# Attention slots of a three-part kernel: the product with v after both passes over the scores

## The chip, the cores and the metric

The kernel runs on one core of one Trainium2 chip. The metric is the time of one execution in device microseconds (us). Five engines work in it: TensorE (PE in the rows, PEld for its weight loads), VectorE (DVE), ScalarE (ACT), GpSimd (POOL) and SyncE (SP), which issues the DMAs.

## What is computed

The reference runs three layers one after the other on 2 batches of 768 tokens. The first is attention over 8 heads of 64 columns, in which a query sees only the keys of its own cluster; the other two are expert layers on the 1536 x 512 result.

```python
def _attn_ref(q, k, v, centroids):
    q_assign = np.argmax(np.einsum('bhsd,hcd->bhsc', q_n, c_n), axis=-1)   # 16 clusters
    k_assign = np.argmax(np.einsum('bhsd,hcd->bhsc', k_n, c_n), axis=-1)
    mask = q_assign[:, :, :, None] == k_assign[:, :, None, :]
    scores = np.where(mask, scale * np.matmul(q, k.transpose(0, 1, 3, 2)), -1000000000.0)
    attn = np.exp(scores - np.max(scores, axis=-1, keepdims=True))
    attn = attn / (np.sum(attn, axis=-1, keepdims=True) + 1e-09)
    return np.matmul(attn, v)

def reference(**kwargs):
    x = attention output, laid out as (B * S, H * D)
    x = _moe_ref(x, w_in, w_out, a, b)        # x @ w_in, a rational function, @ w_out
    return _moe2_ref(x, phi, w1, w2)          # soft mixture of 8 experts
```

Only the attention stage is touched by the change.

## The kernel before

**Pairs and slots.** Two heads make a pair; there are 8 pairs, and each pair takes 12 slots, so the stage has 96 slots, numbered n = 0 to 95 (slot n belongs to pair n // 12, k = n % 12). The loop runs from n = -10 to 96. A pair goes through two passes over its scores. The first pass finds each row's maximum and sum: `a1_mm` (L380 and L381, four matmuls into a two-bank PSUM tile named s1), `a1_neg` (L390 on VectorE: negate, reduce, write to SBUF) and `a1_exp` (L398 on ScalarE: exponential with its row sum). The second pass computes the scores again, transposed and with maximum and sum folded into the operands: `a2_mm` (L455 and L456, four matmuls into a tile s2), `a2_exp` (L460 on ScalarE, which writes e), and then `a2_av` (L469), the product of v and e. The first pass runs LEAD = 10 slots ahead. So a slot n does the second pass of slot n, the first pass of slot n + 10, and the product with v of slot n - 1. Slots 86 to 96 have no first pass left.

**What the two passes share.** The tiles s1 and s2 come in turn from one pool of two buffers (psS): a first pass waits until L390 has read the first pass before it, and a second pass until L460 has read the second pass before it. e and the negated scores have two buffers each, the accumulator of the product with v (psA) one.

**The small work.** Around these, a table of steps by slot (`plan`) prepares the pair three ahead and decodes the 64-bit weights of the next layer. Its steps on TensorE are called small work here: L248 (scores against the centroids), L263 (transposes of them), L290, L306 and L319 (cluster matrices), L434 (statistics of the first pass turned into rows), L601, L610 and L622 (weights of w_out turned and multiplied by phi). Each writes a tile of a pool of three PSUM buffers (psM), which ScalarE or VectorE reads afterwards. L601, L622 and L263 are transposes that fill 128 rows and 128 columns of the array; the others use fewer rows or columns. The step L253 (`scaled`) on ScalarE reads what L248 wrote and stands one slot later in the table.

**The order.** TensorE, ScalarE, VectorE and GpSimd run in the order in which the code emits, and each does its queue in turn; the loop below sets it. The order of SyncE's DMAs is made by the scheduler. Steps of ScalarE, VectorE and GpSimd of a slot are emitted ahead of its second pass by `run`, those of TensorE (the small work) by `run(n, "P")` at the slot's end. At the end of a half pair (n a multiple of 6) ScalarE also copies the product out of psA (`copy`, L480), and GpSimd splits that copy one or two slots later (L489, L490).

Of the kernel before, what the change touches and what calls it, by code (L numbers as in the profile page):

```python
# [59 lines left out]
def tile_kernel(ctx, tc, qT, kT, v, cenT, cenP, consts, constsb, ab, w_in, w_out, phi, w1, w2, out, dbg=None):  # L60
# [85 lines left out]
    def load(p, names="kq"):  # L146
        b, hp = divmod(p, H // 2)
        r = raws.setdefault(p, {})
        for h in range(2):
            for n in names:  # L150
                if (p, n) == (1, "k"):

                    r[n, h] = dec_p.tile([128, 512, 2], I32, tag="raw64", name="rawk1", bufs=2) \
                        .rearrange("p n t -> p (n t)").bitcast(F32)[:, 0:S]
                else:
                    r[n, h] = raw_p.tile([128, S], F32, tag="raw" + n, name=f"raw{n}{h}", bufs=4 if n == "q" else 2)
                SP.dma_start(r[n, h], (kT if n == "k" else qT)[b, 2 * hp + h])

    def load_v(p):
        b, hp = divmod(p, H // 2)  # L160
        vs[p] = v_p.tile([128, 2, 6, D], F32, tag="v", name="vt")
        SP.dma_start(vs[p], v[b, 2 * hp:2 * hp + 2].rearrange("h (j p) d -> p h j d", p=128))
# [299 lines left out]
    def a2_av(p, k):  # L462
        half, j = divmod(k, 6)
        if j == 0:
            av[p, half] = psA.tile([128, 512], F32, tag="av", name="av")
        a = av[p, half]
        e = es.pop((p, k))
        for h in range(2):
            PE.matmul(a[64 * h:64 * h + 64, 0:HS], vs[p][:, h, j, :], e[:, h, :],  # L469
                      start=(j == 0), stop=(j == 5))  # L470

    def a2_x(p, half):

        b, c = divmod(p, H // 2)
        t0 = b * S + half * HS
        hold = {}

        def copy():
            hold["x"] = s2_p.tile([128, HS], F32, tag="x", name="x", bufs=1)
            ACT.copy(hold["x"], av.pop((p, half))[:, 0:HS])  # L480

        def split():
            done = 0
            while done < HS:
                t, off = divmod(t0 + done, TB)
                n = min(HS - done, TB - off)
                src = hold["x"][:, done:done + n]
                dh, dl = xh[t][:, c, off:off + n], xl[t][:, c, off:off + n]
                POOL.tensor_scalar(dh, src, 1.0, 1.0, ALU.mult, ALU.mult)  # L489
                POOL.tensor_tensor(dl, src, dh.bitcast(F32), ALU.subtract)  # L490
                done += n

        return copy, split
# [150 lines left out]
    def open_w():  # L644
        pctx.close()
        keep = ctx.enter_context(tc.tile_pool(name="keep", bufs=1, reuse_waits="tile"))
        return keep, bctx.enter_context(tc.tile_pool(name="wsp", bufs=2 * WAHEAD + 1, reuse_waits="tile"))
# [8 lines left out]
    NSL = 12 * NP  # L656
    plan = {}

    def add(slot, steps):
        for off, eng, fn in steps:  # L660
            plan.setdefault(slot + off, {}).setdefault(eng, []).append(fn)

    def run(slot, engines):
        for eng in engines:
            for fn in plan.get(slot, {}).pop(eng, []):
                fn()
# [25 lines left out]
    for n in range(-LEAD, NSL + 1):  # L692
        p, k = divmod(n, 12)
        if n == -LEAD + 2:
            load_v(0)
        if n == -LEAD + 1:
            load(2, "k")
        if n == -LEAD + 4:
            load(2, "q")
        if n == -5:  # L700
            add(-4, prep(2))
        if n == -2:
            load_v(1)
        if k == 8 and n > 0 and p + 3 < NP:
            add(n, prep(p + 3))
        if k == 1 and 0 < p < NP - 1:
            load_v(p + 1)
        if n > 0 and k == 4 and p + 3 < NP:
            load(p + 3)
        if n == NSL - OPENW:  # L710
            keep, w_p = open_w()
            for i in range(WAHEAD):
                w_load(i)
        run(n, ("S", "A", "D0", "D", "D1", "D2", "G0", "G"))
        if 0 <= n < NSL:
            a2_mm(p, k)
            a2_exp(p, k)
        if n > 0:
            pp, pk = divmod(n - 1, 12)
            a2_av(pp, pk)  # L720
            if pk % 6 == 5:
                copy, split = a2_x(pp, pk // 6)
                copy()
                if n < NSL:
                    add(n + (1 if k else 2), [(0, "G", split)])
                else:
                    split()
        if pend:
            a1_exp(*pend)
            pend = None  # L730
        if n + LEAD < NSL:
            pend = divmod(n + LEAD, 12)
            if n > 0 or n == -LEAD:
                a1_mm(*pend)
            a1_neg(*pend)
            if n < 0:

                a1_mm(*divmod(n + 1 + LEAD, 12))
        run(n, "P")
        if n < -1:  # L740
            idle(2)
    DVE.tensor_scalar(ncoef, coef, -1.0, None, ALU.mult)
# [349 lines left out]
    for c0, cw in COLS:  # L1092
        ne = 256 // cw
        so = bank()
        for e in range(E):
            wt = W["w2", e - e % ne, c0][0][:, (e % ne) * 8 * cw:]
            for kk in range(8):
                k = kk % 4
# [61 lines left out]
```

## Time and profile before

| | us |
|---|---|
| median of 3 runs | 616.59 (615.26 to 618.9) |
| the profiled execution | 617.3 |
| span of its trace | 615.5 |
| slot 1's second pass to the first matmul of the next layer | 43.3 to 336.0 |
| slot 1's second pass to slot 86's, the first slot without a first pass | 43.3 to 314.5 |

TensorE is busy for 561.0 us of the span (91%), VectorE for 463.8 (75%), ScalarE for 392.6 (64%), GpSimd for 375.4 (61%). Between 100 and 300 us VectorE is busy for 43.1, 42.0, 42.9 and 44.1 of each 50 us, TensorE for 46.3 to 47.9. TensorE's granted clock is at full speed in all of the attention stage. A slot takes 2.5 to 4.0 us. In the rows further down, the time in the first column counts from the span's start, the second is the duration; a matmul's end is a model, so distances between starts are the safer numbers. In square brackets stands the idle time of the engine just before, and what ended it.

### The profile page before, as it was taken

How to read it: one execution, taken by the hardware profiler on the slowest of the kernel's cores; microseconds unless marked ns; L12 is line 12 of the kernel's file. 1: busy time of each engine (PE TensorE's matmuls, PEld its weight loads, DVE VectorE, ACT ScalarE, POOL GpSimd, SP SyncE). 2: the span in 40 equal slices, each digit the busy share in tenths (PEclk: the TensorE clock that was granted, in tenths of full speed). 3: DMA queues.
4: the chain of work that ended last, by engine and by line, in shares of the span. 5: the costliest groups of instructions: out<-in, count | busy, mean ns of one | idle time of the engine just before them, and what ended most of it. 6: DMA issues, size and time to landing. Idle time of an engine off the chain costs nothing.

```text
span 615.5 us, 9920 instructions
## 1 busy us (share of the span) xinstructions
PE 561.0 (91%) x3351; PEld 346.1 (56%) x3354; DVE 463.8 (75%) x812; ACT 392.6 (64%) x709; POOL 375.4 (61%) x485
## 2 busy tenths in 40 slices
PE   7899999999999999999999999979899999779973
PEld 2455555555555555555555766756677767423552
DVE  5789698797987979879971799979799979721231
ACT  3687677677776786877874777757677867510110
POOL 8759897996978979887673656534465545301000
PEclk9999999999999999999999999989999999979986
DMA  8804563534635343344334856764747453579998
GB/s 231 224 25 145 161 188 115 170 102 169 192 127 155 117 158 115 116 116 165 117 123 137 295 190 222 269 250 176 270 141 274 132 176 121 211 291 349 307 290 262
DMA packets 83090, 113.77 MB, mean 185 GB/s; under 512 B 17632, under 2 KB 55456, under 8 KB 82528
## 3 DMA queue, kind: packets, MB, share of 16 engines
q1 hardware_dynamic: 83040, 113.14, 56.7%
q8 instruction: 26, 0.43, 0.3%
q14 instruction: 24, 0.20, 0.1%
HBM read 96.02 MB, written 15.73 MB: 182 GB/s over the span
## 4 chain that ended last, share of the span: by engine, by line
PE 50%; DVE 23%; DMA 7%; ACT 7%; issue 6%; POOL 6%; SPq 1%; DVEq 0%; POOLq 0%; ACTq 0%
DVE neg L390 5%; PE s L380 5%; PE h L818 4%; PE h L815 4%; DMA w<-w_in 4%; PE h L816 4%; PE av L469 4%; PE s L455 4%; PE s L381 3%; PE s L456 3%; DMA wt<-w 2%; PE pb L1026 2%; DVE mh L564 2%; ACT neg L398 2%; PE dg L924 2%
## 5 line engine op out<-in xcount | busy, mean ns | idle before, releaser
L390 DVE TENSOR_SCALAR_CACHE_REDUCE neg<-s 128x768 f32<-128x768 f32 x96 | 91.2, 951 | 36.1 <-ACT neg L398 25.2
L460 ACT ACTIVATE e<-s 128x768 f32<-128x768 f32 x96 | 77.5, 807 | 58.3 <-PE s L456 58.2
L398 ACT ACTIVATE neg<-neg,nv 128x768 f32<-128x768 f32 x96 | 89.5, 932 | 9.4 <-DVE neg L390 9.2
L831 POOL TENSOR_SCALAR q<-u,babs 128x512 f32<-128x512 f32 x48 | 41.5, 866 | 82.9 <-ACT u L829 82.9
L380 PE MATMUL s<-k,q 128*128 128x384 f32 x192 | 75.6, 394 | 13.5 <-DVE neg L390 9.9
L469 PE MATMUL av<-e,vt 128*64 128x384 f32 x384 | 83.2, 512 | 0.2 <-ACT e L460 0.2
L815 PE MATMUL h<-xh,w 128*128 128x512 f32 x192 | 80.8, 421 | 0.0
L816 PE MATMUL h<-xl,w 128*128 128x512 f32 x192 | 75.9, 395 | 0.0
L380 PEld LDWEIGHTS s<-k,q 128*128 128x128 f32 x192 | 36.2, 189 | 68.6 <-DVE neg L390 27.4
L455 PE MATMUL s<-q,k 128*128 128x384 f32 x192 | 73.1, 381 | 0.7 <-DVE neg L390 0.5
L833 POOL TENSOR_TENSOR q<-q,u 128x512 f32<-128x512 f32 x48 | 63.9, 1331 | 4.0
L381 PE MATMUL s<-k,q 80*128 80x384 f32 x192 | 65.0, 338 | 0.0
L456 PE MATMUL s<-q,k 128*128 128x384 f32 x192 | 64.7, 337 | 0.0
L818 PE MATMUL h<-xh,w 128*128 128x512 f32 x192 | 53.8, 403 | 5.8 <-DMA w<-w_in 5.8
L579 POOL TENSOR_TENSOR w<-mh,ex 128x512 f32<-128x512 f32 x32 | 44.0, 1374 | 11.2 <-DVE ex L574 5.8
L832 DVE TENSOR_TENSOR p<-p,h 128x512 f32<-128x512 f32 x48 | 32.7, 681 | 22.7 <-ACT p L830 22.5
L840 ACT ACTIVATE r<-q,epsc 128x512 f32<-128x512 f32 x48 | 33.2, 692 | 24.1 <-POOL q L833 23.3
L829 ACT ACTIVATE u<-h 128x512 f32<-128x512 f32 x48 | 28.4, 591 | 28.6 <-PE h L818 28.5
L815 PEld LDWEIGHTS h<-xh,w 128*128 128x128 f32 x192 | 36.2, 189 | 17.5 <-issue 9.3
L818 PEld LDWEIGHTS h<-xh,w 128*128 128x128 f32 x192 | 36.4, 192 | 15.9 <-DMA w<-w_in 7.3
L455 PEld LDWEIGHTS s<-q,k 128*128 128x128 f32 x192 | 36.1, 188 | 16.2 <-issue 8.3
L849 DVE SCALAR_TENSOR_TENSOR p<-q,p 128x512 f32<-128x512 f32 x48 | 44.6, 932 | 0.2
(187 smaller groups left out, 1216.2 us busy)
## 6 DMA issues: line engine op xcount, KB each, us to landing
w<-w_in SPq DMA_DIRECT2D x96, 256.0 KB, 3.2
wt<-w SPq DMA_DIRECT2D x24, 1024.0 KB, 8.1
raw<-w_in SPq DMA_DIRECT2D x16, 512.0 KB, 3.9
raw<-w_out SPq DMA_DIRECT2D x16, 512.0 KB, 3.3
w_in<-w SPq DMA_DIRECT2D x16, 512.0 KB, 2.7
wt<-w SPq DMA_DIRECT2D x16, 512.0 KB, 7.2
rawk<-kT SPq DMA_DIRECT2D x14, 384.0 KB, 3.9
rawq<-qT SPq DMA_DIRECT2D x14, 384.0 KB, 3.6
```

The lines of the kernel that those rows point to most:

```text
L380: PE.matmul(ps[:, c, 0:HS], o["q1"][:, it], o["k1"][:, w], start=True, stop=False)
L381: PE.matmul(ps[:, c, 0:HS], o["q2"][0:80, it], o["k2"][0:80, w], start=False, stop=True)
L390: DVE.tensor_scalar(neg, s1s.pop((p, idx))[:, :, 0:HS], -1.0, None, ALU.mult, ALU.min, accum_out=nvs[p, half][0][:, 0, col:col + 1])
L398: ACT.activation(neg, neg, AF.Exp, scale=-1.0, bias=nv[:, 0, col:col + 1], accum_out=ssum[:, col:col + 1])
L455: PE.matmul(ps[:, h, 0:HS], o["k1"][:, jt], o["q1"][:, w], start=True, stop=False)
L456: PE.matmul(ps[:, h, 0:HS], o["k2"][:, jt], o["q2"][:, w], start=False, stop=True)
L460: ACT.activation(e, s2s.pop((p, k))[:, :, 0:HS], AF.Exp)
L469: PE.matmul(a[64 * h:64 * h + 64, 0:HS], vs[p][:, h, j, :], e[:, h, :], start=(j == 0), stop=(j == 5))
L815: PE.matmul(h, wh[:, c, :], xh[t][:, c, :], start=(c == 0), stop=False)
L816: PE.matmul(h, wh[:, c, :], xl[t][:, c, :], start=False, stop=False)
L818: PE.matmul(h, wl[:, c, :], xh[t][:, c, :], start=False, stop=(c == NCC - 1))
L833: POOL.tensor_tensor(q, q, u, ALU.mult)
```

## The change

The block that emits the product with v (and at the end of a half pair ScalarE's copy and the booking of GpSimd's split) moves from behind the second pass to the end of the slot's body, behind the small work. On TensorE a slot goes from second pass, product with v, first pass, small work to second pass, first pass, small work, product with v. No instruction is added or taken away, and no buffer changes.

```diff
@@ -715,7 +715,20 @@
         if 0 <= n < NSL:
             a2_mm(p, k)
             a2_exp(p, k)
+        if pend:
+            a1_exp(*pend)
+            pend = None
+        if n + LEAD < NSL:
+            pend = divmod(n + LEAD, 12)
+            if n > 0 or n == -LEAD:
+                a1_mm(*pend)
+            a1_neg(*pend)
+            if n < 0:
+
+                a1_mm(*divmod(n + 1 + LEAD, 12))
+        run(n, "P")
         if n > 0:
+
             pp, pk = divmod(n - 1, 12)
             a2_av(pp, pk)
             if pk % 6 == 5:
@@ -725,18 +738,6 @@
                     add(n + (1 if k else 2), [(0, "G", split)])
                 else:
                     split()
-        if pend:
-            a1_exp(*pend)
-            pend = None
-        if n + LEAD < NSL:
-            pend = divmod(n + LEAD, 12)
-            if n > 0 or n == -LEAD:
-                a1_mm(*pend)
-            a1_neg(*pend)
-            if n < 0:
-
-                a1_mm(*divmod(n + 1 + LEAD, 12))
-        run(n, "P")
         if n < -1:
             idle(2)
```

Lines behind this block move down by one in the changed kernel.

**A slot with little small work.** TensorE in slot 28, from the last matmul of its second pass to the first of slot 29's. s1 and s2 are the tiles of the first and second pass, q1, q2, k1, k2 their operands, stat1 the statistics, av the accumulator of the product with v. Before:

```order
L456 MATMUL s2_1605<-q2_2_1_137,k2_2_1_139 128x384
L469 MATMUL av_1485<-e_1563,vt_1032 64x384 x2
L380 MATMUL s1_1615<-k1_0_0_118,q1_0_0_116 128x384
L381 MATMUL s1_1615<-k2_0_0_119,q2_0_0_117 128x384
L380 MATMUL s1_1615<-k1_0_0_118,q1_0_0_116 128x384
L381 MATMUL s1_1615<-k2_0_0_119,q2_0_0_117 128x384
L434 LDWEIGHTS stat1_141
L434 MATMUL mb_1622<-cb_114,stat1_141 32x128
L434 LDWEIGHTS stat1_141
L434 MATMUL mb_1622<-cb_114,stat1_141 32x128
L455 MATMUL s2_1628<-q1_2_0_132,k1_2_0_134 128x384
```

The same stretch now:

```order
L456 MATMUL s2_1605<-q2_2_1_137,k2_2_1_139 128x384
L380 MATMUL s1_1613<-k1_0_0_118,q1_0_0_116 128x384
L381 MATMUL s1_1613<-k2_0_0_119,q2_0_0_117 128x384
L380 MATMUL s1_1613<-k1_0_0_118,q1_0_0_116 128x384
L381 MATMUL s1_1613<-k2_0_0_119,q2_0_0_117 128x384
L434 LDWEIGHTS stat1_141
L434 MATMUL mb_1620<-cb_114,stat1_141 32x128
L434 LDWEIGHTS stat1_141
L434 MATMUL mb_1620<-cb_114,stat1_141 32x128
L469 MATMUL av_1498<-e_1563,vt_1032 64x384 x2
L455 MATMUL s2_1628<-q1_2_0_132,k1_2_0_134 128x384
```

The product with v (of the same e_1563) has gone from between the passes to between the small work and the next second pass.

**A slot whose small work waits for ScalarE.** TensorE in slot 34, from the end of the first pass on. W and oT belong to the cluster matrices, rawq and rawk are the loaded queries and keys of the pair three ahead, cT the centroids. Before:

```order
L381 MATMUL s1_1815<-k2_0_0_119,q2_0_0_117 128x384
L434 LDWEIGHTS stat0_140
L434 MATMUL mb_1822<-cb_114,stat0_140 32x128
L434 LDWEIGHTS stat0_140
L434 MATMUL mb_1822<-cb_114,stat0_140 32x128
L319 LDWEIGHTS W_1650
L319 MATMUL mf_1825<-oT_1596,W_1650 128x384
L248 MATMUL mf_1827<-rawq0_1589,cT_112 32x384
L248 MATMUL mf_1827<-rawq1_1593,cT_112 32x384
L248 MATMUL mf_1827<-rawk0_1587,cT_112 32x384
L248 MATMUL mf_1827<-rawk1_1591,cT_112 32x384
L455 MATMUL s2_1842<-q1_2_0_132,k1_2_0_134 128x384
```

Now:

```order
L381 MATMUL s1_1813<-k2_0_0_119,q2_0_0_117 128x384
L434 LDWEIGHTS stat0_140
L434 MATMUL mb_1820<-cb_114,stat0_140 32x128
L434 LDWEIGHTS stat0_140
L434 MATMUL mb_1820<-cb_114,stat0_140 32x128
L319 LDWEIGHTS W_1650
L319 MATMUL mf_1823<-oT_1596,W_1650 128x384
L248 MATMUL mf_1825<-rawq0_1589,cT_112 32x384
L248 MATMUL mf_1825<-rawq1_1593,cT_112 32x384
L248 MATMUL mf_1825<-rawk0_1587,cT_112 32x384
L248 MATMUL mf_1825<-rawk1_1591,cT_112 32x384
L469 MATMUL av_1708<-e_1775,vt_1032 64x384 x2
L455 MATMUL s2_1842<-q1_2_0_132,k1_2_0_134 128x384
```

The small work is the same; the product with v now stands behind it, and no longer ahead of the first pass whose last matmul is the first row.

**ScalarE at the end of a half pair.** Slot 18 and the first of slot 19. x is the copy of the product, ex a decode step, nh a step of the cluster matrices. Before:

```order
L460 ACTIVATE e_1223<-s2_1218 128x768
L480 COPY x_1227<-av_1050 128x384
L398 ACTIVATE neg_1202,ssum_1090<-neg_1202,nv_1089 128x768
L567 ACTIVATE ex_1211<-ex_1211,epsc_66 128x512
L311 ACTIVATE nh_1242<-mf_1237,cst_64 64x384
L460 ACTIVATE e_1252<-s2_1247 128x768
```

Now:

```order
L460 ACTIVATE e_1223<-s2_1218 128x768
L398 ACTIVATE neg_1200,ssum_1088<-neg_1200,nv_1087 128x768
L480 COPY x_1239<-av_1063 128x384
L567 ACTIVATE ex_1211<-ex_1211,epsc_66 128x512
L311 ACTIVATE nh_1242<-mf_1233,cst_64 64x384
L460 ACTIVATE e_1252<-s2_1247 128x768
```

The copy has changed places with the exponential of the first pass. VectorE's and GpSimd's rows stand in the same order in both kernels; on SyncE the loads of v (L162) slip by one place.

## Rows read from the trace of the kernel before

**Rows 1.** The page: span, and the engines' shares of the chain.

```profile
span 615.5 us, 9920 instructions
PE 50%; DVE 23%; DMA 7%; ACT 7%; issue 6%; POOL 6%; SPq 1%; DVEq 0%; POOLq 0%; ACTq 0%
```

**Rows 2.** Chain that ended last, 126 to 166 us: start, length, engine, tile, line.

```profile
126.61 0.44 PE s L380
...
135.16 1.04 DVE q L441 x2
...
141.98 0.44 PE s L380
...
150.99 0.81 ACT e L460
...
152.72 0.48 ACT sc L253
...
153.24 0.85 PE mf L248 x8
...
156.82 0.96 DVE neg L390 x2
```

**Rows 3.** Timeline of TensorE, slots 28 to 30: start, duration, line, operation, out<-in.

```profile
133.70 0.33 PE L381 MATMUL s<-k,q 80*128 80x384 f32 x1
133.97 0.28 PE L434 MATMUL mb<-cb,stat 128*32 128x128 bf16 x2
134.18 0.44 PE L455 MATMUL s<-q,k 128*128 128x384 f32 x1
...
134.81 0.34 PE L456 MATMUL s<-q,k 128*128 128x384 f32 x1
135.08 0.87 PE L469 MATMUL av<-e,vt 128*64 128x384 f32 x4
135.87 0.45 PE L380 MATMUL s<-k,q 128*128 128x384 f32 x1
...
136.51 0.34 PE L381 MATMUL s<-k,q 80*128 80x384 f32 x1
...
137.22 0.34 PE L456 MATMUL s<-q,k 128*128 128x384 f32 x1
```

**Rows 4.** Timeline of TensorE, slots 49 to 51: what follows full transposes.

```profile
201.40 0.60 PE L601 MATMUL mf<-cst,w 128*128 128x128 f32 x4
...
201.75 0.42 PE L455 MATMUL s<-q,k 128*128 128x384 f32 x1
...
207.91 0.60 PE L622 MATMUL mf<-cst,wph 128*128 128x128 f32 x4
...
208.45 0.52 PE L290 MATMUL mb<-cb,eq 128*64 128x128 bf16 x6
```

**Rows 5.** Timeline of slot 34: the small work that waits for ScalarE.

```profile
152.80 0.33 PE L319 MATMUL mf<-oT,W 64*128 64x384 bf16 x1
...
153.24 0.11 PEld L248 LDWEIGHTS mf<-rawq,cT 64*32 64x32 f32 x2 [0.35 <-ACT sc L253]
```

**Rows 6.** Timeline of slots 36 to 40: VectorE beside GpSimd, and the statistics.

```profile
161.77 1.91 POOL L258 TENSOR_TENSOR k<-rawk,k 64x768 fp32r<-64x768 f32 x1
...
161.90 2.33 DVE L570 SCALAR_TENSOR_TENSOR mh<-raw,mh 128x512 f32<-128x512 uint32 x1
...
170.21 0.68 DVE L570 SCALAR_TENSOR_TENSOR mh<-raw,mh 128x512 f32<-128x512 uint32 x1
...
171.34 0.24 POOL L429 TENSOR_TENSOR stat<-r,stat 128x12 bf16<-128x12 f32 x1
...
172.07 0.28 PE L434 MATMUL mb<-cb,stat 128*32 128x128 bf16 x2
```

**Rows 7.** Timeline of the slots without first pass: the last turned weights.

```profile
325.39 0.66 PE L601 MATMUL mf<-cst,w 128*128 128x128 f32 x4 [0.94 <-POOL w L579]
```

**Rows 8.** The tile av, its reader: engine, operation, count, duration in ns.

```profile
L480 ACT COPY x<-av x16: 478/479/480, 60.4 to 336.2; 128x384 f32<-128x384 f32 x16
```

More of the change, by code (lines that the diff above doesn't have):

```diff
@@ L717, in tile_kernel @@
             a2_exp(p, k)
[L718 to L727, printed above, removed]
         if pend:
@@ L739, in tile_kernel @@
         run(n, "P")
+        if n > 0:
+            pp, pk = divmod(n - 1, 12)
+            a2_av(pp, pk)
+            if pk % 6 == 5:
+                copy, split = a2_x(pp, pk // 6)
+                copy()
+                if n < NSL:
+                    add(n + (1 if k else 2), [(0, "G", split)])
+                else:
+                    split()
         if n < -1:
```

## The prediction

> **What bounds the kernel now.** I read the page first: TensorE carries half of the chain that ended last, VectorE a quarter of it, in a span of 615.5 us [rows 1]. Then the chain itself over one pair's twelve slots [rows 2]; there the reader is to see that the two engines take turns. From 126.61 us to 135.16 TensorE is the chain (slots 26 to 28), then VectorE; from 141.98 to 150.99 TensorE again (slots 31 to 34), then ScalarE until it gives way to a matmul at 153.24, TensorE once more, and from 156.82 VectorE until slot 38. This pattern comes back five times, in the pairs whose slots prepare another one (small work L248 in slots 10, 22, 34, 46, 58). A saving on TensorE counts only in TensorE's stretches; in VectorE's it becomes a longer wait. Last I read the distances between matmul starts in these stretches [rows 3 to 5].
>
> **What the change leaves alone.** Nothing is added or removed. In a cycle, first pass, small work, product, second pass is the old order turned round by one place: between two first passes stand the same things as before, and between two second passes too. So a first pass gets the same time from the one before it for L390, and a second pass for L460; neither wait grows by itself. The wait of the product for e gets longer cover. What changes is what stands next to what, and that the second pass (with ScalarE behind it) comes later against the first pass and the small work.
>
> **Neighbours on TensorE.** Take the loop round L434 [rows 3], from the last matmul of a first pass to the last of the next: 133.70 to L434 0.27, to the second pass 0.21, to its last matmul 0.63 (134.81), to the product 0.27, to the first pass 0.79, to its last matmul 0.64: 2.81 us. Where a pass follows a pass, last to last is 0.71 (136.51 to 137.22). The changed loop is 0.27 to L434, then the product at an unknown distance, 0.79 and 0.64 for the second pass behind it, 0.71 for the first pass: 2.41 plus the unknown one. Bounds for that: 0.21, what L434 needs ahead of a second pass, and 0.27, what a product needs behind a pass; below, 0, if a narrow product could start beside narrow small work. I take 0.21, since the row is of the same small work: 2.62, a gain of 0.19. A slot without small work gains nothing: 0.71 + 0.27 + 0.79 + 0.64 in either order. Nor does one that ends in full transposes: a second pass comes 0.35 after their first (201.40 to 201.75), a narrow product 0.54 (207.91 to 208.45) [rows 4], which takes the 0.19 back. By the order of the code, 47 of the slots 1 to 85 end in narrow small work, 25 in transposes, 13 have none.
>
> Of the 47, those in TensorE's stretches count. In the first kind (slots 26 to 28) two loops lie, in the second (31 to 34) two besides the one priced next, and in the late slots (67 to 75) three. Over five pairs and the late slots: 5 x 2 x 0.19 = 1.9, 5 x 2 x 0.19 = 1.9 and 3 x 0.19 = 0.57 us gained.
>
> The Trainium skill has a rule that speaks against this gain: "TensorE: Matmul & The Clock Gate", section "Part 3: Packing small matmuls — row/col tiling", says that a weight load overlaps a running matmul only when it goes to other rows of the array. By it passes in a row would hide no weight loads, and the sum would be worse by the 4.4 us that the gains amount to. The 0.71 between two joined passes, against 0.63 and 0.64 behind anything else, is against it.
>
> **L248 in slots 10, 22, 34, 46, 58.** It needs a buffer that L253 on ScalarE frees, and L253 stands behind the exponentials of the slot: e starts at 150.99, L253 at 152.72, L248 follows at 153.24, 2.25 us after e's start [rows 2]. Its distance from the small work ahead of it is 0.44 (152.80 to 153.24) [rows 5] where 0.27 is usual behind a wide product [rows 3], so it already waits 0.17. Now the small work comes earlier by what stood between the passes: 0.27 + 0.79 + 0.64 = 1.70 becomes 0.71, 0.99 less, and the wait becomes 1.16 us. Against the clock: the product with v of slot 33 now stands ahead of the second pass of slot 34 and moves it, ScalarE's 2.25 us and L248 by 0.79 us. So five times 0.79 is lost, 3.95 us. Between nothing (were the wait covered) and 5 x 1.16 = 5.8 us I take 3.95, since both distances are rows of the place.
>
> **Once per kernel.** At the first wait that ends TensorE's lead, one product with v that was done ahead of a first pass is now still to do: 0.79 us, once. In the slots without first pass, L601 at 325.39 waits for GpSimd's L579 [rows 7], whose chain starts behind the last a1_exp, in ScalarE's queue behind an e that now comes one product later: another 0.79; bounds 0 (if GpSimd has slack there) and 1.6.
>
> **The other queues.** ScalarE's copy (0.48 us, 16 times [rows 8]) now waits for the slot's end; behind it stand a decode step, in half the cases L311, and the next e. What hides it is TensorE's next second pass and, where there is one, its wait for L390; without that cover it costs up to 16 x 0.48 = 7.7 us. I take 0: no wait of a second pass for e is in the chain's rows, and ScalarE holds 7% of the chain [rows 1]. VectorE and GpSimd keep their orders. SyncE's loads of v wait for the last product of a pair, which comes up to one slot's rest later, and the loads of raw keys, queries and weights behind them with them; their data are used three or more slots on, so 0, and if not, at most that 1 us a pair.
>
> **The sum.** -1.9 - 1.9 - 0.57 + 3.95 + 0.79 + 0.79 = +1.2 us. The profiled execution took 617.3 us, 0.7 above the median of the runs, so 618.5 there and **617.8 us** as a median: no change that can be measured (0.5% of 616.6 is 3.1 us, about what a measurement of this kernel can tell from none: 613.5 to 619.7).
>
> **Rivals.** *Faster, by VectorE.* Beside GpSimd's L258 the decode step L570 takes 2.33 us, elsewhere 0.68; it starts 0.13 us after L258 [rows 6]. It lies at the end of VectorE's stretch of slots 36 and 37, ahead of the first pass's L390. GpSimd's chain there begins behind a ScalarE step, which comes up to 0.99 later against the first passes. If L258 then starts behind L570, up to 1.65 us goes, five times: 617.8 - 8.2 = 609.6; half of it, where TensorE is next in line, 613.7; together some 612. For it: only 0.13 decides, and all five pairs have the same phase. Against it: VectorE comes later too, and L570 may meet the GpSimd instruction ahead of L258. The Trainium skill, "SBUF — State Buffer", section "Who interferes with whom", has the mechanism: whichever of the two starts first keeps the shared port for its whole instruction. The trace agrees: L570 ends 0.55 us behind L258's end (161.77 + 1.91), little less than it takes alone.
>
> *Slower, by GpSimd.* The statistics are ready (L429, 171.34 + 0.24) 0.49 us ahead of L434 at 172.07 [rows 6]. If GpSimd's chain comes the full 0.99 later there, L434 waits 0.5 us, in up to five pairs, and VectorE's L441 behind it opens the stretch that ends at the next wait: +2.5. A VectorE step that newly runs into a two-input step of GpSimd costs another 1.65 where it lands in such a stretch; in one or two pairs of five that is 2 to 3 us. 617.8 + 2.5 = 620.3, up to 623. It decides from a lateness of 0.49 on. For it: the margin is half of the lateness. Against it: the chain leaves TensorE right behind this L434 at 135.16 [rows 2], so that a short wait there may be covered by VectorE's own work.
>
> *Slower, by the weights.* If joined passes hid nothing, the 4.4 us of gains would go: 622.2. The 0.71 speaks against it.
>
> *Nothing moves.* If the waits of TensorE for L390 swallow gain and loss alike, 616.6.
>
> **How the numbers follow.** Forecast and "nothing moves", both within 0.5%: 0.40 and 0.10. Faster by VectorE: 0.20. Slower by GpSimd: 0.27, by the weights: 0.03. So faster by over 0.5% 0.20, within 0.50, slower 0.30. The range leaves out the ends of both sides: 611.5 to 622.5. Its lower end also holds the unknown distance at 0 (23 loops x 0.21 = 4.8 us less, 613.0), its upper end the 0.27 (1.4 us more).
>
> **What would show it.** In the new trace a slot with narrow small work and no wait should be 0.19 us shorter, from 2.81 to 2.62 in the loop round L434, and the last matmul of a second pass should be 0.71 from that of the first pass behind it. L248 in slot 34 should wait over 1 us for L253, and slot 34 to 35 last some 0.6 longer. L570 at 2.33 or near 0.7, and L434 waiting for L429 or not, tell the rivals apart. The prediction is wrong if second passes wait for e at the half pairs, if the product behind small work starts at once, or if VectorE's stretches change by more than a microsecond each.

## The result, and the profile after

The changed kernel takes 622.74 us (median of four runs, 621.42 to 624.51) against 615.92 us of the kernel before beside it: 1.012 times as long, 95% interval 1.0082 to 1.0157. The prediction was 617.8 us in a range of 611.5 to 622.5, and "no change" as the likeliest sign. It is 6.8 us slower where 1.2 was forecast, just above the range. The profiled execution took 621.64 us.

In the attention stage the profile shows more than that: the first matmul of the next layer comes at 344.3 us instead of 336.0. The stage behind it, which the change does not touch, took 275.6 us here and 279.5 before, and from 275 to 289 us in the 20 executions profiled for this study. So a run's time is blurred by a stage that has nothing to do with the order; the cause is looked for in the attention stage, slot by slot, in the one traced execution that each kernel has.

The page of after, to set beside [rows 1]: span, and the engines' shares of the chain that ended last.

```profile
span 619.9 us, 9919 instructions
PE 47%; DVE 18%; POOL 14%; DMA 8%; ACT 6%; issue 5%; SPq 1%; POOLq 0%; DVEq 0%; ACTq 0%
```

GpSimd's share went from 6% to 14%. That is the new thing.

The neighbours on TensorE came out as priced. Timeline of TensorE in after, slots 28 and 29, the stretch of [rows 3]:

```profile
134.64 0.33 PE L381 MATMUL s<-k,q 80*128 80x384 f32 x1
134.91 0.28 PE L434 MATMUL mb<-cb,stat 128*32 128x128 bf16 x2
135.12 0.87 PE L469 MATMUL av<-e,vt 128*64 128x384 f32 x4
135.92 0.44 PE L455 MATMUL s<-q,k 128*128 128x384 f32 x1
...
136.54 0.35 PE L456 MATMUL s<-q,k 128*128 128x384 f32 x1
...
137.26 0.33 PE L381 MATMUL s<-k,q 80*128 80x384 f32 x1
```

From the last matmul of one first pass to that of the next it is 2.62 us (134.64 to 137.26), 2.81 before; L434 to the product 0.21; pass to pass 0.72. And L248 in slot 34, the place of [rows 5]:

```profile
153.99 0.33 PE L319 MATMUL mf<-oT,W 64*128 64x384 bf16 x1
155.43 0.51 PE L248 MATMUL mf<-rawq,cT 64*32 64x384 f32 x2 [1.11 <-ACT sc L253]
```

The distance is 1.44 us, and 0.26 without a wait (e1, below): a wait of 1.18 us, where 1.16 was forecast. These distances came out as priced, and the time was still wrong.

**Where a period goes.** The pattern repeats every twelve slots. I cut a period at two instructions of GpSimd: L417, the first step of the statistics of a half pair that needs the logarithm from ScalarE (slot 32), and the end of L579 in slot 42. Two views of busy time, each of the stretch from L417 to L579's end and of the stretch from there to the next L417 (slot 44): stretch and its length, then each engine's busy time, the granted clock, the DMA's share. Before:

```profile
146.82:179.74 32.92, 31.29 (x174) 17.89 (x174) 28.16 (x54) 24.10 (x44) 30.50 (x44) 1.00 0.47 152
179.74:185.79 6.05, 5.62 (x36) 3.45 (x37) 4.98 (x10) 5.09 (x11) 2.18 (x3) 1.00 0.40 144
```

After:

```profile
149.23:182.20 32.97, 29.50 (x169) 17.63 (x168) 28.29 (x50) 22.28 (x41) 30.54 (x43) 1.00 0.45 140
182.20:189.07 6.87, 6.45 (x40) 4.12 (x41) 5.19 (x12) 6.35 (x13) 2.34 (x4) 1.00 0.53 179
```

The reader is to see that the first part is the same within 0.05 us, although it holds all of L248's wait and most of TensorE's gains. GpSimd is at work for 30.5 us of it, and apart from the 0.43 us ahead of L417 it waits for no other engine. The second part, the way back from GpSimd to GpSimd, is 0.82 us longer. What lies on it, from the chain of waits (start, length, engine, tile, line). Before:

```profile
178.59 1.43 DVE mh L564
180.02 0.88 DVE neg L390 x2
...
180.95 0.44 PE s L380
...
181.93 0.44 PE mf L601 x4
182.37 0.18 PE s L455
```

After:

```profile
181.08 1.41 DVE mh L564
182.49 0.89 DVE neg L390 x2
...
183.41 0.44 PE s L380
...
184.39 0.44 PE mf L601 x4
184.83 0.80 PE av L469 x4
185.62 0.37 PE s L455
```

A piece of the chain begins where the piece ahead of it ends, so distances are taken from the timelines, where an instruction stands with its own start. TensorE, ScalarE and GpSimd before:

```profile
182.12 0.42 PE L455 MATMUL s<-q,k 128*128 128x384 f32 x1
...
182.88 0.57 ACT L311 ACTIVATE nh<-mf,cst 64x384 fp32r<-64x384 f32 x1
183.36 0.79 ACT L460 ACTIVATE e<-s 128x768 f32<-128x768 f32 x1
...
185.16 0.20 POOL L416 TENSOR_SCALAR s<-ssum 128x6 f32<-128x6 f32 x1 [3.36 <-ACT neg L398]
```

The same in after, TensorE and ScalarE first, then GpSimd:

```profile
185.55 0.44 PE L455 MATMUL s<-q,k 128*128 128x384 f32 x1
...
186.63 0.81 ACT L460 ACTIVATE e<-s 128x768 f32<-128x768 f32 x1 [0.31 <-PE s L456]
187.34 0.93 ACT L398 ACTIVATE neg<-neg,nv 128x768 f32<-128x768 f32 x1
...
188.39 0.30 ACT L406 ACTIVATE l<-ssum,epsc 128x6 f32<-128x6 f32 x1
188.72 0.21 ACT L407 ACTIVATE l<-l 128x6 f32<-128x6 f32 x1
```

```profile
188.44 0.20 POOL L416 TENSOR_SCALAR s<-ssum 128x6 f32<-128x6 f32 x1 [3.46 <-ACT neg L398]
189.07 0.32 POOL L417 TENSOR_TENSOR l<-s,l 128x6 f32<-128x6 f32 x1 [0.43 <-ACT l L407]
```

So it is a ring. VectorE's L564 in slot 42 cannot go on until GpSimd's L579 ends; L390 stands behind L564, the first pass of slot 43 waits for L390, then come small work and the second pass of slot 44, its exponential, the last L398 of the half behind it in ScalarE's queue, the logarithm, and GpSimd starts again. **TensorE enters the ring by a first pass and leaves it by a second pass.** In the old order nothing but small work lies between, in the new one a product with v as well. From the first matmul of the first pass to that of the second it is 1.17 us before (180.95 to 182.12) and 2.14 after (183.41 to 185.55), 0.97 more: the product's 0.79, and nearly 0.2 that a narrow product loses behind full transposes [rows 4]. To the exponential L460 it is 2.41 before (to 183.36) and 3.22 after (to 186.63), 0.81 more, since before, L460 stood behind L311 in ScalarE's queue and hid 0.16.

That VectorE waits there for GpSimd shows only in a duration. All instructions of L564 in the kernel before (count, duration in ns: least, median, most):

```profile
L564 DVE TENSOR_SCALAR mh<-raw x32: 415/726/1515, 43.2 to 317.7; 128x512 int32<-128x512 int32 x32
```

Its least is 0.41 us. In slot 42 it is 1.50 before and 1.48 after, and it ends 0.28 us behind L579's end in both kernels, in after in each of the five periods. The Trainium skill, "SBUF — State Buffer", section "Who interferes with whom", counts a tensor_scalar, but for the form that also writes out its accumulator, among the steps that can take VectorE's second port pair, which GpSimd shares, and says that who starts first keeps it for the whole instruction. The trace agrees: L579 starts 0.53 us ahead of L564, and L390, of the excepted form, keeps to 0.93 to 0.96 us all 96 times in both kernels (it also reads from PSUM, and no run here tells which of the two keeps it clear).

The stage adds up, second pass to second pass, after less before: slots 1 to 8 +0.83, the five periods to slot 68 +0.90, +1.08, +0.86, +0.85 and +1.85, slots 68 to 86 +1.05, to slot 95 +1.09, and -0.23 at slot 1: +8.28 us. The longer way back is 5 x 0.82 = 4.1 us of it. The last of the five periods lost 1.0 more at the low clock (L417 to L579's end 33.72 us, 32.69 before).

### The profile page after: what moved, and what is told of

Its sections match the earlier page's. It is cut to its first block, busy times and chain, and to the rows that moved or that the text cites. A ratio compares the mean times of both kernels' runs of the same rounds, so it can differ in the third digit from the quotient of the medians.

```text
span 619.9 us, 9919 instructions
## 1 busy us (share of the span) xinstructions
PE 557.8 (90%) x3354; PEld 350.9 (57%) x3354; DVE 464.7 (75%) x812; ACT 389.1 (63%) x709; POOL 375.8 (61%) x485
## 4 chain that ended last, share of the span: by engine, by line
PE 47%; DVE 18%; POOL 14%; DMA 8%; ACT 6%; issue 5%; SPq 1%; POOLq 0%; DVEq 0%; ACTq 0%
PE av L469 6%; DMA w<-w_in 4%; PE s L455 4%; PE h L816 4%; PE h L819 4%; PE s L380 4%; DVE neg L390 4%; PE h L817 3%; PE s L381 3%; PE pb L1027 3%; PE s L456 2%; DMA wt<-w 2%; POOL w L579 2%; DVE mh L564 2%; POOL q L332 2%
## 5 line engine op out<-in xcount | busy, mean ns | idle before, releaser
L460 ACT ACTIVATE e<-s 128x768 f32<-128x768 f32 x96 | 77.6, 808 | 75.1 <-PE s L456 75.1
L390 DVE TENSOR_SCALAR_CACHE_REDUCE neg<-s 128x768 f32<-128x768 f32 x96 | 91.3, 953 | 35.7 <-PE s L381 30.1
L398 ACT ACTIVATE neg<-neg,nv 128x768 f32<-128x768 f32 x96 | 89.1, 928 | 4.6 <-DVE neg L390 3.9
L380 PE MATMUL s<-k,q 128*128 128x384 f32 x192 | 69.5, 362 | 18.0 <-DVE neg L390 12.7
L455 PE MATMUL s<-q,k 128*128 128x384 f32 x192 | 76.1, 396 | 0.1
L456 PE MATMUL s<-q,k 128*128 128x384 f32 x192 | 65.7, 342 | 0.0
L579 POOL TENSOR_TENSOR w<-mh,ex 128x512 f32<-128x512 f32 x32 | 44.4, 1386 | 11.2 <-DMA w_out<-w 5.9
L833 DVE TENSOR_TENSOR p<-p,h 128x512 f32<-128x512 f32 x48 | 32.7, 682 | 21.6 <-ACT p L831 21.4
```

What stands on the lines that cost most here:

```text
L380: PE.matmul(ps[:, c, 0:HS], o["q1"][:, it], o["k1"][:, w], start=True, stop=False)
L390: DVE.tensor_scalar(neg, s1s.pop((p, idx))[:, :, 0:HS], -1.0, None, ALU.mult, ALU.min, accum_out=nvs[p, half][0][:, 0, col:col + 1])
L398: ACT.activation(neg, neg, AF.Exp, scale=-1.0, bias=nv[:, 0, col:col + 1], accum_out=ssum[:, col:col + 1])
L455: PE.matmul(ps[:, h, 0:HS], o["k1"][:, jt], o["q1"][:, w], start=True, stop=False)
L456: PE.matmul(ps[:, h, 0:HS], o["k2"][:, jt], o["q2"][:, w], start=False, stop=True)
L460: ACT.activation(e, s2s.pop((p, k))[:, :, 0:HS], AF.Exp)
```

## The experiments

Parts of a period (us) in one period in which the clock stayed up; "low" counts the stretches of slots 1 to 96 in which the granted clock fell to 0.5 (1.2 GHz). Times are ratios to the kernel before on the same chip.

| kernel | L417 to L579 | way back | period | low | time | 95% |
|---|---|---|---|---|---|---|
| before | 32.92 | 6.05 | 38.97 | 0 | 1 | |
| after | 32.97 | 6.87 | 39.83 | 2 | 1.012 | 1.008 to 1.016 |
| e1 | 33.03 | 6.85 | 39.88 | 4 | 1.022 | 1.016 to 1.029 |
| e2 | 32.77 | 6.05 | 38.82 | 0 | 1.000 | 0.996 to 1.003 |
| e3 | 33.04 | 6.31 | 39.36 | 1 | 1.012 | 1.007 to 1.018 |
| e4 | 32.71 | 6.87 | 39.57 | 3 | 1.011 | 1.007 to 1.015 |
| e5 | 32.82 | 5.76 | 38.58 | 1 | 1.004 | 1.001 to 1.007 |
| e6 | 34.20 | 6.05 | 40.25 | 4 | 1.023 | 1.017 to 1.029 |
| e7 | order differs | | 38.72 | 6 | 1.017 | 1.013 to 1.022 |
| e8 | 33.14 | 4.34 | 37.48 | 3 | 1.001 | 0.998 to 1.005 |
| e9 | 33.05 | 6.87 | 39.92 | 6 | 1.021 | 1.017 to 1.026 |
| e10 | 32.68 | 6.46 | 39.14 | 4 | 1.018 | 1.012 to 1.024 |
| e11 | 32.82 | 6.69 | 39.50 | 1 | 1.017 | 1.012 to 1.022 |
| e12 | 33.16 | 5.50 | 38.67 | 2 | 1.005 | 1.002 to 1.009 |
| e13 | 32.99 | 6.44 | 39.43 | 2 | 1.012 | 1.007 to 1.016 |
| e14 | 33.10 | 6.87 | 39.97 | 5 | 1.017 | 1.013 to 1.021 |
| e15 | 33.18 | 5.75 | 38.93 | 6 | 1.012 | 1.007 to 1.017 |
| e16 | 33.37 | 5.36 | 38.73 | 0 | 0.997 | 0.994 to 1.000 |
| e17 | 31.44 | 6.86 | 38.30 | 2 | 1.000 | 0.996 to 1.003 |
| e18 | 30.79 | 7.38 | 38.17 | 1 | 0.993 | 0.989 to 0.997 |

The first column is the finding: with the same GpSimd work (all but e6, e17 and e18; e7 puts it in another order) it is 32.7 to 33.4 us in these periods, whatever TensorE and ScalarE do. In e8, e11, e17 and e18 periods of two lengths alternate; the row has a short one, the long ones last 38.6, 40.3, 39.1 and 38.7 us.

**Is it L248's wait? e1, and e2 on the kernel before.**

```
-            (3, "A", lambda: scaled(0)),
+            (2, "A", lambda: scaled(0)),
```

In the table, `scaled(0)` stands two slots behind the L248 whose scores it reads, and one behind the L248 that waits for its buffer; the edit takes one slot away.

> The changed kernel with the ScalarE step L253 of the first scores tile (scaled(0)) booked one slot earlier, so that it stands ahead of the second pass's exponential and no longer behind it; nothing else is moved. Changed kernel: 1.012 of before. Theory A (the wait of L248 for L253 in slots 10, 22, 34, 46, 58 is the loss, 5 x 1.2 us, and the TensorE clock that falls behind two of these waits comes from them): the wait goes, the granted clock stays at full speed in the attention stage, and the time falls to before's or below it, 0.995 to 1.002. Theory B (the later exponentials of the first pass put GpSimd's queue of a half pair on the path, and that sets how long a period of twelve slots lasts): the wait of L248 goes but the time comes back as waits for GpSimd and VectorE; 1.006 to 1.012, GpSimd still at over 10% of the chain.

> The kernel before with the same edit (scaled(0) one slot earlier). There L248 waits only 0.17 us in each of five slots. Both theories: 0.997 to 1.001. It is the control for e1: what e1 gains beyond this belongs to the changed order.

In e1 the wait is gone. Timeline of its TensorE in slot 22, the place that answers to slot 34:

```profile
110.64 0.33 PE L319 MATMUL mf<-oT,W 64*128 64x384 bf16 x1
110.90 0.51 PE L248 MATMUL mf<-rawq,cT 64*32 64x384 f32 x2
```

0.26 us instead of 1.44. Yet this period lasts 39.88 us, as in after (39.89 there, with a stretch at the low clock in it, and 39.83 the next). Against the next one, from slot 32 on, e1 is 1.18 us ahead from the end of slot 22 to slot 25, and level again at slot 27. Timeline of e1's VectorE in slots 24 and 25:

```profile
123.82 1.00 DVE L280 TENSOR_TENSOR eq<-eq,cb 128x384 bf16<-128x384 bf16 x1
124.75 2.32 DVE L570 SCALAR_TENSOR_TENSOR mh<-raw,mh 128x512 f32<-128x512 uint32 x1
126.99 0.94 DVE L390 TENSOR_SCALAR_CACHE_REDUCE neg<-s 128x768 f32<-128x768 f32 x1
```

TensorE and VectorE arrive earlier at GpSimd's L257 and L258 and stand there longer. Theory A falls: the wait of L248 lies beside GpSimd's queue. That e1 is even slower than the changed kernel was not expected. It has twice as many stretches at the low clock, on which more below; but in the traces its attention stage ends only 1.25 us later than that of after, and most of the difference lies in the stage behind. e2 changed nothing, as expected.

**Is it the start of the statistics? e3, e5.** e3, and what e5 adds to it:

```
+        if pend:
+            a1_exp(*pend)
+            pend = None
         if 0 <= n < NSL:
             a2_mm(p, k)
             a2_exp(p, k)
-        if pend:
-            a1_exp(*pend)
-            pend = None
```

```
-        return [(0, "A", log)] + [(0, "G0", lambda a=a: parts(a)) for a in range(6)] + [(1, "P", rows), (2, "D0", place)]
+        return [(-1, "B", log)] + [(0, "G0", lambda a=a: parts(a)) for a in range(6)] + [(1, "P", rows), (2, "D0", place)]
...
+        run(n, ("B",))
```

with the last line right behind `a1_exp`.

> The changed kernel with the exponential of the first pass (L398) ahead of the second pass's (L460) in ScalarE's queue of a slot; ScalarE stands idle there, since it waits for the second pass. So the statistics of a half pair and GpSimd's queue behind them start some 0.8 to 1.0 us earlier; L253 stays behind both exponentials, so that L248 still waits about 1.2 us in five slots. Theory A (L248's wait is the loss): no change against the changed kernel, 1.010 to 1.014, granted clock still falling twice. Theory B (GpSimd's queue, started by the last L398 of a half, is the path): 1.000 to 1.006, GpSimd back from 14% to some 6% of the chain.

> e3 with one thing more: the logarithm L406, L407 of a half pair stands right behind the last exponential L398 of the half and ahead of the second pass's L460 (in e3 it stood behind it, and GpSimd's second step L417 waited for it). So L417 starts some 0.8 to 1.0 us earlier than in e3, 1.4 us or more earlier in its slot than in the changed kernel. Theory B (a ring: GpSimd's unbroken queue from the statistics of one half to a step that VectorE or TensorE waits for, and from there back to the next statistics; it sets the period of twelve slots, 39.83 us in the changed kernel, 39.35 in e3): the period falls by about what L417 gains, to 38.9 or less, 0.996 to 1.004 of before. Rival C (another engine's order sets the 39.3): period 39.2 to 39.4 as in e3, 1.008 to 1.013.

The way back fell from 6.87 to 6.31 and 5.76 us, the period by 0.47 and 1.25. That fits the ring, and in e5 the attention stage ends at 337.1 us instead of 344.3 with TensorE still in the new order. In time e5 is 1.004, inside what was expected; e3 is 1.012, above the 1.006. Against before, both lose 2 to 3 us in slots 1 to 8, with a stretch at the low clock among it, which I did not take apart.

**Does it close at qa or at L434? e4, e7.** e4 has the first of these edits, e7 both:

```
-            qa = hold["qa", h, c] = s2_p.tile([128, HS], F32, tag="qa", name="qa")
+            qa = hold["qa", h, c] = s2_p.tile([128, HS], F32, tag="qa", name="qa", bufs=4)
...
-                    add(n + (1 if k else 2), [(0, "G", split)])
+                    add(n + (1 if k else 3), [(0, "G", split)])
```

> The changed kernel with four buffers instead of two for the tile qa, so that VectorE's L323 no longer waits until GpSimd's L332 has read the tile two before it (7 waits, 7.4 us of VectorE's idle time after, at slots of kind 17 and 18 where each period loses 0.5 to 0.6 us). Theory B in its narrow form (this wait is where GpSimd's queue meets the path): 5 x 0.55 = 2.8 us less, 1.006 to 1.009. Theory A, or GpSimd meeting the path at L434 instead: 1.011 to 1.013.

> e4 (four buffers for qa) with the split L489, L490 of the first half (2.4 us of GpSimd) one slot later, behind the statistics and L258 instead of ahead of them. So the statistics that L434 of slot 40 waits for are ready 2.4 us earlier, while GpSimd meets VectorE in slots 35 to 38 at the same distances. Theory B with the ring closed at L434: period from 39.8 to 39.0 or less, 0.997 to 1.005. Theory B with the ring closed by VectorE beside GpSimd (slots 34 to 37: L570 against L258, whose port they share): no gain, 1.009 to 1.013.

In e4 the seven waits of L323 are gone, and it keeps 39.6 to 39.8 in four periods of five (the other, 40.5, has the low clock on its way back): not there. e7 is mixed: its two periods with an undisturbed clock are 38.5 and 38.7, the others 39.2 to 40.1. It has six stretches at the low clock, and its 1.017 lies above both expectations. In the undisturbed one from slot 44 on L564 ends 1.15 us ahead of L579's end, so the ring is cut; but the edit moves too much of GpSimd's queue to tell L434 from L579.

**The converse: more GpSimd work in the kernel before, e6.**

```
             POOL.tensor_scalar(q2[0:64, w], qa[0:64, :], 1.0, 1.0, ALU.mult, ALU.mult)
+            if c == 0:
+                POOL.tensor_scalar(q2[0:64, w], qa[0:64, :], 1.0, 1.0, ALU.mult, ALU.mult)
```

> The kernel before with GpSimd's step L331 done twice for the first half of each query (two more steps of 0.5 to 0.8 us in twelve slots, same values written again), nothing else. GpSimd is idle for 3.8 us of such a period there, ahead of the statistics in slot 32. Theory B: the slack of the ring in the kernel before is 0.3 to 0.5 us, so that the period grows by 0.7 to 1.0 us, from 38.95 to 39.7 or more; 1.006 to 1.010, and GpSimd goes from 6% to over 10% of the chain. Rival (GpSimd's idle time covers it, it is no bound): 0.998 to 1.002.

Busy time by stretch in e6, cut at L417 and L579 as above:

```profile
109.47:143.66 34.19, 31.73 (x178) 18.36 (x178) 29.53 (x55) 24.23 (x44) 31.63 (x46) 1.00 0.46 145
143.66:149.72 6.06, 5.63 (x36) 3.46 (x37) 4.99 (x10) 5.10 (x11) 2.19 (x5) 1.00 0.43 150
```

The first part grows by 1.3 us, the way back stays. 1.1 us more of GpSimd work, with 3.8 us of idle time in the period, comes out in full: the kernel before stands on the ring too, with no slack at all (0.3 to 0.5 had been expected). The time, 1.023, is far above the expected 1.010; the three later periods have the low clock and last 41.1 to 41.7 us.

**In which slot? e9, e10, e13, e14.** `product()` is the moved block; in e9 and e13 it stands between the passes again in one slot of twelve (k = 6, k = 7), in e10 and e14 it is moved behind the small work in that slot alone:

```
+        if k == 7:
+            product()
...
+        if k != 7:
+            product()
```

> The changed kernel with the old order in one slot of twelve: in slots 6, 18, 30, 42, 54, 66, 78, 90 the product with v (and ScalarE's copy) stands between the passes again. Theory D (what theory B says of GpSimd's queue, with the place where the change lengthens the ring: TensorE enters it by the first pass of slot 42, which waits for VectorE, which waits for GpSimd's second L258, and leaves it by the second pass of slot 44, whose exponential the last L398 and the statistics stand behind; in the new order two products with v lie between, in the old one): the period of twelve slots falls by up to one product, 0.79 us, from 39.83 to 39.0 to 39.2 where the clock stays up, L248 still waits 1.2 us, 1.000 to 1.005 of before. Any theory in which the loss is spread over the slots, or is L248's wait: 39.7 or more, 1.010 to 1.013.

> The converse of e9: the kernel before with the new order in slots 6, 18, 30, 42, 54, 66, 78, 90 alone. Theory D: this one slot carries most of the loss; the period grows from 38.97 by 0.6 to 0.8 us, to 39.6 to 39.8, 1.005 to 1.009. Any other theory so far: one slot of twelve costs nothing, 0.998 to 1.002.

> The changed kernel with the old order (product with v between the passes) in slots 7, 19, 31, 43, ... alone. Theory E: the ring is GpSimd's unbroken queue from L417 of slot 32 to L579 of slot 42, VectorE's L564 that waits for it, L390, the first pass of slot 43, then one product with v that the new order puts here, the second pass of slot 44, its exponential, the last L398 of the half, the statistics. Without that product the period falls from 39.83 by 0.79 to 39.0 to 39.1 where the clock stays up, while L248 still waits 1.2 us and all other slots are in the new order; 1.001 to 1.006 of before. A loss that is spread over the slots, or L248's wait: 39.7 or more, 1.010 to 1.013.

> The converse of e13: the kernel before with the new order in slots 7, 19, 31, 43, ... alone. Theory E: this one slot in twelve costs as much as the whole change, the period grows from 38.97 by 0.7 to 0.8 us to 39.7 to 39.8; 1.005 to 1.009 of before. Otherwise 38.9 to 39.0, 0.999 to 1.001.

e9 failed: 39.92, no gain. TensorE is held once more behind slot 42, at the first pass of slot 43, so a product in slot 42 is covered. That gave theory E. e14 bears it out: the new order in slot 43 alone makes the way back 6.87 us, all that the whole change does. Two periods of e14, each in its two stretches:

```profile
112.72:145.82 33.10, 31.93 (x177) 18.46 (x176) 28.47 (x55) 24.19 (x44) 30.67 (x44) 1.00 0.42 131
145.82:152.69 6.87, 5.66 (x35) 3.38 (x36) 4.79 (x8) 5.21 (x11) 2.17 (x4) 1.00 0.48 170
152.69:185.81 33.12, 31.48 (x173) 17.97 (x172) 28.36 (x54) 24.09 (x44) 30.70 (x44) 1.00 0.45 142
185.81:194.22 8.41, 7.21 (x35) 4.12 (x36) 4.79 (x8) 5.20 (x11) 2.17 (x4) 0.80 0.59 183
```

The period is 39.97 where the clock stays up, 0.2 above what was expected, and 41.0 to 41.5 where it falls (0.80 in the fourth row); this happens in four periods and once ahead of them. The traced execution took 636.6 us, the longest of six with a median of 628.4, so the 1.017 (1.005 to 1.009 expected) need not stand for as many. e13 gave half of what was expected: the way back is 6.44, not 6.05. First to second pass is as short as before again (1.17 us), but the first pass of slot 43 now comes 0.30 later behind L564: with slot 42 in the new order and slot 43 in the old, two products lie between their first passes, 4.11 us of TensorE where L390 asks for 3.8. In e13's trace the attention stage ends 3.8 us earlier than in after, though its time is no better. e10's 4.12 in the same place is that again: its way back is 6.46, so the new order in slot 42 alone costs 0.4 as well; the one period with the clock up is 39.14 where 39.6 to 39.8 was expected, and the four others have the low clock.

**Versions: e8, e11, e12, e15, e16.** e8 is e5 with e1's edit and e7's split; e12 is e5 with e1's and e9's; e11 is the kernel before with e5's order on ScalarE; e15 is e13 with e1's edit and, for the first half in slots k = 8 alone, e5's order; e16 is the kernel before with that last edit alone:

```
+        if pend and k == 8:
+            a1_exp(*pend)
+            pend = None
+            run(n, ("B",))
         if 0 <= n < NSL:
```

> e5 with scaled(0) one slot earlier (e1) and the split one slot later (e7, with two buffers for qa). If the GpSimd ring is what the changed order costs, and L248's wait shows again once the ring has slack, this has the TensorE gains of the changed order alone: some 0.2 us in 8 to 9 slots of each period less what VectorE's stretches take, period 37.5 to 38.5, 0.987 to 0.997 of before. If VectorE's stretches bind at the same period: 0.998 to 1.004.

> The kernel before (old order on TensorE) with e5's order on ScalarE: exponential of the first pass and logarithm ahead of the second pass's exponential. If GpSimd's ring sets the period in the kernel before too (L570 and L574 are held by L258 there as well), the statistics come 0.4 us earlier in their slot and the period falls from 38.97 to 38.5 to 38.6; 0.994 to 0.999. If it is not the ring there: 0.999 to 1.003.

> The changed order but for slots 6, 18, 30, ... (e9), with e5's order on ScalarE and scaled(0) one slot earlier (e1). By theory D the ring is some 1.1 + 0.8 us shorter than in the changed kernel: period 37.7 to 38.2 where the clock stays up, 0.988 to 0.998 of before. If it is bound elsewhere or loses TensorE's clock in its waits: 0.998 to 1.004.

> e13 with two things more: in slots 8, 20, 32, 44, ... alone the last exponential L398 of the half and the logarithm stand ahead of the second pass's exponential (in e5 in every slot, which cost up to 3 us in the first slots), and scaled(0) is one slot earlier. Theory E: the ring is 0.8 us shorter than in e13 by the product and 1.0 to 1.1 by ScalarE's order: period 37.9 to 38.2, 0.988 to 0.998 of before. If something else binds by then: 38.5 or more, 0.999 or above.

> The kernel before, old order on TensorE, with ScalarE's order of e15 in slots 8, 20, 32, 44, ... alone. If the ring sets the period there too, L417 comes up to 0.8 us earlier in its slot and the period falls from 38.97 to 38.2 to 38.6; 0.992 to 0.998. If not: 0.999 to 1.001.

e8 has the shortest periods, 37.48 and 38.60 in turn, but lost 3 us in slots 1 to 8 and 3 in slots 76 to 86 and came out level. e11, e12 and e15 missed: e11's way back is no shorter (6.69 and 7.2 in turn), and L564 in slot 42 starts 0.6 us behind L579's end there and takes 0.4, so it is another path; e12 has 38.7 where 37.7 to 38.2 was expected, e15 lost its clock six times and has one clean period, 38.93. e16 was faster, 615.47 against 617.06 us, 0.9967 (0.9937 to 0.9997): the only version with all the work that beats both kernels, and narrowly. Its way back is 5.36 instead of 6.05; 0.4 of the 0.7 us went into the first part (33.37), so by then the ring binds less than it did. In its profiled execution the attention stage ends at 336.1 us, no earlier than before: the clock fell once ahead of slot 1, which cost 1.6 us.

**With less GpSimd work: e17, e18.** The line of L332 is left out in both orders.

> The changed kernel without GpSimd's step L332 (the low part of q for the other half of the rows, four times in twelve slots, 1.0 us each); scores lose that part of the precision, nothing else is left out. GpSimd's queue from L417 to L579 is some 4 us shorter and the ring can no longer close. Theory E: the period falls well below 39.0, and against e18 the order then costs what the prediction summed for its own terms (per period some 1.0 of L248's wait less 0.2 for each of four to five slots): e17 over e18 0.998 to 1.004. If the order costs without the ring too: e17 over e18 1.008 or more.

> The kernel before without the same four GpSimd steps. Theory E (the ring sets the period in the kernel before too): the period falls from 38.97 by 1 us or more, 0.97 to 0.993 of before. If VectorE and TensorE set it: 38.6 or more, 0.995 to 1.000.

GpSimd's queue is no longer unbroken in either kernel: in every period an L579 waits for VectorE's L574, 0.69 us in e17 and 1.7 in e18. e18 takes 0.993 of before's time, but its period falls by 0.3 to 0.8 us, 0.4 in the mean of five, and not by the 1 or more that theory E asked for; its attention stage ends 1.5 us earlier, and the rest of the time lies in the stage behind. So the ring does bound the kernel before, but with 4 us of GpSimd work gone something else, which no run here shows, holds the period close behind it.

The five periods to slot 68 average 38.80 us in e17 and 38.47 in e18, 0.33 apart instead of 1.1, and the attention stage ends 1.97 us later instead of 8.3. So with this queue cut the order costs some 2 us of the stage, and the other 6 go with the ring and the clock. That is one execution of each, and the cut is not complete: in three of e17's five periods L564 still ends 0.28 us behind L579, with a way back of 6.86 us as in after. In time e17 stands to e18 as 0.9997 to 0.9927, 1.007, between the 1.004 and the 1.008 that were to tell the cases apart, with both intervals 0.35 to 0.4% wide to a side; it settles neither. That the 2 us are near the +1.2 of the prediction's sum may be chance: they were not taken apart into its terms.

## Why the prediction was wrong

- **Neighbours**: right in size (0.19 a loop, 0.21 to the product, 0.72 between joined passes). The rival of the weights is out. But of the 4.4 us of gains most lie in the first part of the period, which GpSimd sets, and are worth nothing there.
- **L248**: the wait was right to 0.02 us, and the slot grows by 0.79 us, the price (the sign to look for had said 0.6). The 3.95 us made of it was wrong: in the period it costs nothing (e1). That it nearly cancels the gains, which are worth nothing either, is luck.
- **"Once per kernel, 0.79"**: this is the step that failed. It says that a product that was done ahead of a first pass is still to do when TensorE's lead ends. The mechanism was right and the size near (partly by luck: 0.97 on TensorE, of which 0.16 was hidden), but it falls due each time that TensorE is entered by a first pass and left by a second: the way back grows by 0.82 us in each of five periods, 4.1 of the 8.3 us, where 0.79 was counted. Slots 1 to 8 grow by 0.83 too. The prediction did say that the second pass, "with ScalarE behind it", comes later against the first pass; it put no price on what ScalarE then starts later.
- **What bounds the kernel now**: the root of it. The chain showed "DVE" for steps that stood still behind GpSimd. For L570, at 2.33 us [rows 6], the prediction saw this, in the rival "faster by VectorE"; it missed L564 at 1.50, and never asked what starts GpSimd's queue again. Its 3.4 us of idle time ahead of L416 looked like slack; it was part of the ring's way back.
- **Tail**: +0.79 forecast, +1.09 from slot 86 to 95.
- **Other queues**: ScalarE's copy at 0 held here: in after GpSimd's L489 waits 0.56 us for it behind slot 42, and GpSimd stands idle for 3.46 us afterwards all the same.
- **Rivals**: "slower by GpSimd" (620.3 to 623) had the engine, and the time lies in its span, but by luck, since its place was wrong: L434 waits for L429 by no more than 0.14 us. "Faster by VectorE" did not come: in three pairs of five L570 still takes 2.33 us, and starts 0.05 us behind L258's start instead of 0.13. In the other two, behind a stretch at the low clock, it starts after L258's end and takes 0.99 and 1.50 us, and these periods (39.89 and 40.59 us) are no shorter. As far as these two show, the rival's gain would have lain beside the ring as well.

Left open: the 0.83 us of slots 1 to 8 and the 1.05 of slots 68 to 86, what holds the period at 38.5 us in e18, and what lets the clock fall.

## What to carry to other kernels

A step whose duration is several times its least one may be standing still; look for the other engine that was busy when it ended before calling its own engine the bound. Where a pattern repeats, look for the ring: follow the chain until it comes back to the same instruction one period later, and price a reordering by what it puts between the points at which each engine enters and leaves it. A wait beside the ring need not cost anything (here 1.18 us, five times), and a term that looks like once per kernel can fall due once per turn of the ring. The next bound may stand close behind the ring: here cutting 4 us out of it won 0.4.

## What the runs showed of the hardware

TensorE's granted clock fell inside the attention stage, from full speed (2.4 GHz) to 0.5 (1.2 GHz), twice in after and never in before. Busy time in after, slots 21 to 23: ahead of L248's wait, with it, behind it (PE first, the clock third from the end):

```profile
110.00:114.00 4.00, 4.00 (x26) 2.10 (x25) 2.58 (x4) 2.90 (x6) 3.45 (x8) 1.00 0.20 23
114.00:117.20 3.20, 2.09 (x16) 0.53 (x14) 2.09 (x5) 1.48 (x4) 3.03 (x5) 1.00 0.40 164
117.30:120.60 3.30, 3.30 (x11) 2.53 (x11) 1.50 (x3) 1.84 (x4) 3.14 (x4) 0.50 0.53 181
```

In the kernels of this study each such stretch between slots 1 and 86 began 1.2 to 4.1 us after the start of a gap of 1.3 to 2.5 us between two matmul starts: at L248 in after and e13, in slots of the kinds k = 1, 2 and 6 in e1, e6 and e10, in those of kind 7 in e14. Not every such gap had one: three of the five waits of L248 in after did not, nor did a gap of 1.78 us in before, and a gap of 2.3 us in slot 2 had one in e3 and e5 and none in after and e1. On the way back of the ring it costs 1.5 us (e14, 6.87 to 8.41); inside GpSimd's part little for a single one, 33.02 us in after against 32.97 without, and more for one twice as long (33.72). An order that gathers TensorE's idle time into fewer, longer waits may lose here a second time: e1 removed one wait and made the next one 2 us long, and three of its four stretches stand behind such waits.
